# Channel attention with a two-layer feed-forward block: the softmax of batches 1 to 3 without TensorE, and other dues for the loads of the opening

## The chip, the core and the metric

The kernel runs on one core of a Trainium2 chip. Its engines are TensorE (PE, matrix products, with weight loads shown as PEld), VectorE (DVE), ScalarE (ACT), GpSimd (POOL) and SyncE (SP, which here issues every DMA). Each takes its instructions in order, and an instruction that waits holds up those behind it. The metric is the device time of one execution in microseconds (us), the median of several.

## The reference

Per batch, channels attend to channels, and the result goes through a feed-forward block with a piecewise activation. Cut to what matters:

```python
B, N, C = (4, 6080, 256)
qn = q / (np.linalg.norm(q, axis=1, keepdims=True) + 1e-06)
kn = k / (np.linalg.norm(k, axis=1, keepdims=True) + 1e-06)
s = kn.transpose(0, 2, 1) @ qn / tau            # 256 x 256 per batch
s = s - s.max(-1, keepdims=True)
a = np.exp(s)
a /= a.sum(-1, keepdims=True) + 1e-09
x = v @ a                                       # (4 * 6080) x 256
h = x @ w_in                                    # d_ff = 2048
g = np.where(h >= 1, h, np.where(h <= -1, 0.0, (h + 1) ** 2 / 4))
out = g @ w_out
```

`w_in` and `w_out` come as 64-bit floats.

## The kernel before

**What is computed where.** The two products v·a and ·w_in are merged: per batch W = a·w_in is made once, and h = v·W. Every operand of a large product is held as two fp32r parts, and a product is three matmuls (`mm3`, L465 to L469). h = v·W uses a Strassen form with seven products (`strassen`). N is cut into six column pairs per batch, and 2048 hidden channels into eight slices `i` of 256, so there are 48 groups per batch and 192 in all; a group is `h_ops` (the product and the activation) and `o_ops` (the product with `w_out`). Each group's h tiles leave PSUM through ACT and DVE and come back as operands of the `w_out` product.

**Batch 0's opening.** The Gram matrix kᵀq of batch 0 is made from chunks of 512 rows (1 MB each, the first of 256 rows) by plain fp32 matmuls in `big_chunk` (L848), from four buffers `kq_0` to `kq_3`. ACT squares each chunk and DVE adds the squares (L863, L864) for the norms. The first `EARLY` chunks of batch 1 go through the same loop, for the Gram matrix alone. Meanwhile the 64-bit weights are loaded and converted by ACT and DVE (`convert`), the first tiles of v are split (`make_V`), and W of batch 0 is made (`make_W`). `LOADS` places those loads: kind, index, due time, and the chunk load behind whose issue they may start.

**Later batches.** While the groups of one batch run, the rest of the next batch's Gram matrix is made from 256-row pieces (`gram_chunk`, 12 matmuls each on tile `kqs`) and the squares from `square_piece`. In group 40 of 0 to 47 (`SOFT_AT = 8`) comes `softmax(b + 1)`, and in groups 45 and 47 (`W_AT`) `make_W7`, which forms the next batch's W from tile `eT`, the transposed exponentials.

**Inside `softmax` before**, for all batches: DVE sums the squares, POOL takes the root (L527), DVE takes the reciprocals (L532). 1/|q| lies one channel to a partition and is wanted along the free axis in all partitions: DVE makes two diagonal matrices (L537), PE multiplies them by a matrix of ones (L544), DVE copies the result to `rq` (L547). Then scaling (L550), row maxima (L553), exponentials on ACT (L559), four transposes on PE (L569), and for batches 1 to 3 two copies from PSUM to `sf_mem` on ACT (L584), sums on POOL (L675) and the split into `eT` by ACT and DVE (L679, L681).

**What sets the order.** Nothing is issued as it is written: each operation is given to `Order` with an engine, an assumed length, the buffers it reads and writes, and a due time. `Order.run` walks through assumed times and, per engine, takes among the operations that can start the one with the earliest due; if none can start at once, the one that can start first. An urgent one (batch 0's norms and softmax) counts as startable up to `SOON` us ahead, so that the engine waits for it. The result is a fixed order for each engine. So a changed due can move instructions all over the program. Buffers, and with them what a load must wait for, are picked in the same walk.

Of the kernel before, what the change touches and what calls it, by code (L numbers as in the profile page):

```python
# [9 lines left out]
F32 = mybir.dt.float32  # L10
# [5 lines left out]
P = 128  # L16
# [31 lines left out]


URGENT = -1000.0  # L50
SOON = 0.6


class Op:
# [161 lines left out]
def pool_us(n):  # L216
# [20 lines left out]
W_AT = (3, 1)
SUMS_AT = (18, 21, 24, 27)  # L240
SOFT_AT = 8


HEAD = (2,)
KQ0, KQ1 = -12.0, 3.7


LOADS = (("in", 0, 42, 7), ("out", 0, 34, 2), ("in", 1, 42, 5), ("out", 2, 42, 4),
         ("v", 0, 52, 10), ("in", 2, 56, 7), ("out", 4, -46, 6), ("out", 6, 34, 6))


@with_exitstack
def channel_attention_moe(ctx: ExitStack, tc: tile.TileContext, kq, kqT, vT, tau, w_in, w_out, outT):
# [258 lines left out]
    def softmax(b, due):  # L512

        st = sts[b]
        c = st.col = buf("cols")
        col = lambda a, n: c.ap[:, a:a + n]
        ssq, nrm, rn = lambda: col(0, 4), lambda: col(4, 4), lambda: col(8, 4)
        nmax, sums, rs = lambda: col(12, 2), lambda: col(14, 2), lambda: col(16, 2)
        st.rs = rs
        V = nc.vector  # L520
        if b == 0:
            op("DVE", 0.2, lambda: V.tensor_copy(ssq(), st.pt.ap[:, :4]), r=[st.pt], w=[c], due=due)
        else:
            op("DVE", 0.2, lambda: V.tensor_reduce(
                out=ssq(), in_=st.ssq.ap[:, :4 * NCW].rearrange("p (a k) -> p a k", k=NCW), axis=AX.X, op=ALU.add),
               r=[st.ssq], w=[c], due=due)
        op("POOL", 1.0, lambda: nc.gpsimd.tensor_tensor(out=nrm(), in0=ssq(), in1=half, op=ALU.pow), w=[c], due=due)  # L527
        op("DVE", 0.1, lambda: V.tensor_scalar(out=nrm(), in0=nrm(), scalar1=1e-6, scalar2=None, op0=ALU.add), w=[c],
           due=due)
        op("DVE", 0.1, lambda: V.tensor_scalar(out=nrm()[:, :CT], in0=nrm()[:, :CT], scalar1=tau_sb, scalar2=None,  # L530
                                              op0=ALU.mult), w=[c], due=due)
        op("DVE", 0.1, lambda: V.reciprocal(rn(), nrm()), w=[c], due=due)  # L532
        q, s = buf("rq"), buf("sf")
        dg = lambda ct: s.ap[:, ct]
        sv = lambda it: s.ap.rearrange("p (t j) f -> p t (j f)", t=4)[:, it]
        for ct in range(CT):
            op("DVE", 0.25, lambda ct=ct: V.tensor_scalar(out=dg(ct), in0=ident,  # L537
                                                         scalar1=rn()[:, CT + ct:CT + ct + 1], scalar2=None,
                                                         op0=ALU.mult), r=[c], w=[s], due=due)
        z = buf("Z")  # L540

        def scales():
            for ct in range(CT):
                nc.tensor.matmul(z.ap[:, ct * P:(ct + 1) * P], lhsT=ones, rhs=dg(ct), start=True, stop=True)  # L544

        op("PE", 0.7, scales, r=[s], w=[z], due=due + 3)
        op("DVE", 0.42, lambda: V.tensor_copy(q.ap, z.ap[:, :C]), r=[z], w=[q], due=due + 3)  # L547
# [14 lines left out]
        if b == 0:  # L562
            touch(IDENTITY_SAT240, [s], due + 6.1)
        z2 = buf("Z")

        def transposes():
            for it in range(CT):
                for jt in range(CT):
                    nc.tensor.transpose(z2.ap[:, (jt * CT + it) * P:(jt * CT + it + 1) * P],  # L569
                                        sv(it)[:, jt * P:(jt + 1) * P], ident)  # L570

        op("PE", 0.6, transposes, r=[s], w=[z2], due=due + 8)
        if b == 0:
            st.eT = buf("eT")
            eT = lambda a: st.eT.ap[:, a * CT * C:(a + 1) * CT * C].rearrange("p (j c) -> p j c", j=CT)
            zz = lambda: z2.ap.rearrange("p (j c) -> p j c", j=CT)
            op("ACT", act_us(512), lambda: nc.scalar.copy(eT(0), zz()), r=[z2], w=[st.eT], due=due + 9)
            op("DVE", dve_us(512), lambda: V.tensor_tensor(out=eT(1), in0=zz(), in1=f32(eT(0)),
                                                          op=ALU.subtract), r=[z2], w=[st.eT], due=due + 9)
        else:  # L580
            f = s
            st.eT = buf("eT")
            for jt in range(CT):
                op("ACT", act_us(256), lambda jt=jt: nc.scalar.copy(  # L584
                    f.ap[:, OUT_[jt], :], z2.ap[:, jt * C:(jt + 1) * C].rearrange("p (i c) -> p i c", i=CT)),
                   r=[z2], w=[f], due=due + 9)
# [377 lines left out]
```

## Time and profile before

| | before |
|---|---|
| median of 3 runs | 2162.06 us (2161.85 to 2165.43) |
| the profiled execution's own time | 2162.27 us |
| its span in the profile | 2160.5 us |
| ACT busy | 1589.3 us (74%) |
| POOL busy | 246.5 us (11%) |
| bytes moved by DMA | 369.48 MB, mean 171 GB/s |

The span runs from the first to the last instruction; 1.8 us of the execution lie around it. Shares are of the span. In the timelines that follow, the columns are start, length, engine, line, operation, tiles, shape and count, and in brackets the idle time ahead of it and what ended that. A matmul's shown length reaches past the start of the next one, so its cost is read from start to start. A matmul of plain fp32 operands (L848, L544, L569) shows up as two instructions.

### The profile page before, as it was taken

The page shows a single profiled execution, that of the slowest core. Times are in us where ns is not written, and L with a number is a line of the kernel's source. Part 1 is how long each engine was busy: PE and PEld are TensorE (multiplying, and loading weights), DVE is VectorE, ACT ScalarE, POOL GpSimd, SP SyncE. Part 2 cuts the span into 40 slices and gives each one's busy share as a digit, 9 for nine tenths or more (in the row PEclk, how much of TensorE's full clock was granted, in tenths as well). Part 3 has the DMA queues.
Part 4 walks back from the last instruction along what each step waited for, and adds up shares of the span by engine and source line. Part 5 has one row for each costly group of instructions (what it writes and reads, how often), then busy time and mean ns, then how long its engine had stood idle before and what let it go on. Part 6 is the DMA issues. An engine that isn't in the chain of part 4 may idle for free.

```text
span 2160.5 us, 27947 instructions
## 1 busy us (share of the span) xinstructions
PE 2150.3 (100%) x9904; PEld 1804.1 (84%) x9904; DVE 1791.0 (83%) x2917; ACT 1589.3 (74%) x2809; POOL 246.5 (11%) x260
## 2 busy tenths in 40 slices
PE   9999999999999999999999999999999999999999
PEld 7888888888888888888888888888888888888888
DVE  7898888888798888888889888888888887778776
ACT  6687777777788777777777877777777767777776
POOL 0320020100131001000023000000012201001000
PEclk9999999999999999999999999999999999999999
DMA  9755466454665444544456445354455532332331
GB/s 382 289 188 174 144 219 219 164 179 144 200 232 182 171 154 159 181 163 159 173 185 222 172 163 182 144 202 143 150 184 190 185 124 91 128 127 96 121 120 36
DMA packets 115340, 369.48 MB, mean 171 GB/s; under 512 B 10496, under 2 KB 40192, under 8 KB 112768
## 3 DMA queue, kind: packets, MB, share of 16 engines
q1 hardware_dynamic: 115200, 367.70, 48.5%
q8 instruction: 78, 1.28, 0.2%
q14 instruction: 62, 0.51, 0.1%
HBM read 297.67 MB, written 69.99 MB: 170 GB/s over the span
## 4 chain that ended last, share of the span: by engine, by line
PE 96%; DVE 1%; DMA 0%; issue 0%; POOL 0%; ACT 0%; SPq 0%; DVEq 0%; ACTq 0%
PE bank L468 95%; DMA wop_d<-win_mem 0%; PE bank L848 0%; POOL t L719 0%; DVE v L728 0%; DVE v L726 0%; DVE win_mem L406 0%; DVE x L771 0%; PE bank L544 0%; PE bank L569 0%; DVE u_mem L399 0%; DVE wout L406 0%; DVE bank L622 0%; ACT v L725 0%; DVE mh_mem L626 0%
## 5 line engine op out<-in xcount | busy, mean ns | idle before, releaser
L468 PE MATMUL bank<-x,wout 128*128 128x512 f32 (+1 forms) x3948 | 1014.7, 388 | 0.0
L468 PEld LDWEIGHTS bank<-x,wout 128*128 128x128 f32 x3948 | 738.9, 188 | 146.7 <-DVE x L771 0.2
L468 PE MATMUL bank<-v,w_mem 128*128 128x512 f32 (+1 forms) x3264 | 850.1, 388 | 1.5 <-DVE v L728 0.8
L468 PEld LDWEIGHTS bank<-v,w_mem 128*128 128x128 f32 x3264 | 610.0, 188 | 125.4 <-DVE v L728 1.9
L763 ACT ACTIVATE u_mem<-bank 128x512 f32<-128x512 f32 (+1 forms) x576 | 341.8, 593 | 269.0 <-PE bank L468 259.1
L767 DVE TENSOR_TENSOR u_mem<-bank,u_mem 128x512 f32<-128x512 f32 (+1 forms) x576 | 390.6, 679 | 126.6 <-ACT u_mem L765 125.1
L765 ACT ACTIVATE u_mem<-u_mem 128x512 f32<-128x512 f32 (+1 forms) x768 | 469.1, 625 | 7.2
L771 DVE TENSOR_TENSOR x<-u_mem,x 128x512 fp32r<-128x512 f32 (+1 forms) x658 | 459.8, 706 | 11.4 <-ACT x L769 7.3
L769 ACT CAST x<-u_mem 128x512 fp32r<-128x512 f32 (+1 forms) x284 | 173.8, 615 | 78.7 <-DVE u_mem L767 78.2
L622 DVE TENSOR_TENSOR bank<-bank,mh_mem 128x512 f32<-128x512 f32 (+1 forms) x198 | 137.0, 692 | 96.4 <-PE bank L468 95.9
L468 PE MATMUL bank<-x,w_mem 128*128 128x512 f32 (+1 forms) x768 | 208.5, 388 | 0.0
L468 PE MATMUL bank<-g,wout 128*128 128x512 f32 (+1 forms) x660 | 183.4, 387 | 0.0
L719 POOL TENSOR_TENSOR t<-raw_mem 128x512 f32<-128x512 f32 (+1 forms) x48 | 66.8, 1392 | 890.0 <-DMA raw_mem<-vT 294.3
L468 PEld LDWEIGHTS bank<-x,w_mem 128*128 128x128 f32 x768 | 143.7, 188 | 28.8 <-DVE bank L622 0.2
L770 DVE CAST x<-u_mem 128x512 fp32r<-128x512 f32 (+1 forms) x374 | 159.5, 435 | 8.5 <-DVE u_mem L767 0.5
L626 DVE TENSOR_TENSOR mh_mem<-bank,mh_mem 128x512 f32<-128x512 f32 (+1 forms) x198 | 135.4, 684 | 37.4 <-PE bank L468 32.5
L617 ACT COPY mh_mem<-bank 128x512 f32<-128x512 f32 (+1 forms) x198 | 115.3, 582 | 65.1 <-PE bank L468 62.6
L767 DVE TENSOR_TENSOR u_mem<-mh_mem,u_mem 128x512 f32<-128x512 f32 (+1 forms) x192 | 136.4, 711 | 13.3 <-ACT u_mem L765 13.0
L468 PEld LDWEIGHTS bank<-g,wout 128*128 128x128 f32 x660 | 123.5, 188 | 24.5 <-DVE g L771 0.2
L619 ACT COPY bank<-bank 128x512 f32<-128x512 f32 (+1 forms) x198 | 113.3, 572 | 33.8 <-PE bank L468 28.3
L763 ACT ACTIVATE u_mem<-mh_mem 128x512 f32<-128x512 f32 (+1 forms) x192 | 119.0, 620 | 7.0 <-DVE mh_mem L626 6.8
L719 POOL TENSOR_TENSOR t<-raw_mem,t 128x512 f32<-128x512 f32 (+1 forms) x48 | 67.3, 1402 | 460.5 <-DVE v L728 369.2
(104 smaller groups left out, 1452.8 us busy)
## 6 DMA issues: line engine op xcount, KB each, us to landing
w_mem<-w_d SPq DMA_DIRECT2D x160, 896.0 KB, 4.6
raw_mem<-kqT SPq DMA_DIRECT2D x60, 512.0 KB, 6.1
w_d<-w_mem SPq DMA_DIRECT2D x32, 896.0 KB, 4.5
raw_mem<-kq SPq DMA_DIRECT2D x53, 512.0 KB, 5.5
raw_mem<-vT SPq DMA_DIRECT2D x40, 512.0 KB, 6.5
outT<-y_mem SPq DMA_DIRECT2D x80, 256.0 KB, 2.6
kq<-kq SPq DMA_DIRECT2D x19, 1024.0 KB, 9.0
win_mem<-wop_d SPq DMA_DIRECT2D x21, 512.0 KB, 5.7
```

The lines of the kernel that those rows point to most:

```text
L468: nc.tensor.matmul(out, lhsT=lhs(a), rhs=rhs(c), start=start and m == 0, stop=stop and m == 2, skip_group_check=skip)
L617: op("ACT", act_us(n), lambda: nc.scalar.copy(m5.ap[:, :n], a.ap[:, :n]), r=[a], w=[m5], due=early)
L619: op("ACT", act_us(n), lambda: nc.scalar.copy(a.ap[:, :n], z.ap[:, :n]), r=[z], w=[a], due=early)
L622: op("DVE", dve_us(n), lambda: nc.vector.tensor_tensor(out=bb.ap[:, :n], in0=z.ap[:, :n], in1=m5.ap[:, :n], op=ALU.add), r=[z, m5], w=[bb] ...
L626: op("DVE", dve_us(n), lambda: nc.vector.tensor_tensor(out=h22.ap[:, :n], in0=z.ap[:, :n], in1=m5.ap[:, :n], op=ALU.add), r=[z, m5], w=[h2 ...
L719: op("POOL", pool_us(n), lambda: nc.gpsimd.tensor_tensor(out=tt(x), in0=a(), in1=c(), op=ALU.subtract), r=r, w=[ts[x]], due=due + d, gates ...
L763: op("ACT", act_us(n), lambda: nc.scalar.activation(us(), src(), IDENTITY_SAT240, scale=240.0), r=[h], w=[u], due=d_sat)
L765: op("ACT", act_us(n), lambda: nc.scalar.activation(us(), us(), AF.Square, bias=0.5, scale=1.0 / 480.0), w=[u], due=d_sq)
L767: op("DVE", dve_us(n), lambda: nc.vector.tensor_tensor(out=us(), in0=src(), in1=us(), op=ALU.max), r=[h], w=[u], due=d_max)
L769: op("ACT", act_us(n), lambda: nc.scalar.copy(t.ap[:, 0, :n], us()), r=[u], w=[t], due=d_hi, other=("DVE", dve1_us(n), lambda: nc.vector.t ...
L770: other=("DVE", dve1_us(n), lambda: nc.vector.tensor_copy(t.ap[:, 0, :n], us())) if g >= FIRST else None)
L771: op("DVE", dve_us(n), lambda: nc.vector.tensor_tensor(out=t.ap[:, 1, :n], in0=us(), in1=f32(t.ap[:, 0, :n]), op=ALU.subtract), r=[u], w=[ ...
```

## The change

For batches 1 to 3 the spreading of 1/|q| goes through memory: SP stores the 256 reciprocals (4 bytes each) to a DRAM row `rn_d`, and loads that row into all partitions of `rq`. The exponentials are transposed in blocks of 32 x 32 by DVE into a `u` buffer, stored by eight DMAs that put the blocks in their places in `e_d` (256 runs of 128 bytes each), and loaded by two DMAs into `sf_mem`, where the copies from PSUM went. The two PE steps, the copy to `rq`, and the two ACT copies per batch go. Batch 0 keeps them. Beside it, planner numbers change: `SOON`, the number of early chunks of batch 1 (8 to 9), from which group on DVE may take ACT's casts, and dues and gates of several loads.

```diff
-SOON = 0.6
+SOON = 0.3
...
-EARLY = 8
+EARLY = 9
-FIRST = 0
+FIRST = 4
...
-SLACK = 0.0
-WOP_DUE, W_DUE, TAKE_DUE = -48, -14, -20
-GRAM_END = 0
-KQS_J = (2, 3)
+SLACK = 0
+WOP_DUE, W_DUE, TAKE_DUE = -60, -14, -20
+GRAM_END = 1
+KQS_J = (4, 5)
 W_AT = (3, 1)
-SUMS_AT = (18, 21, 24, 27)
-SOFT_AT = 8
+SUMS_AT = (20, 23, 28, 31)
+SOFT_AT = 9
...
-KQ0, KQ1 = -12.0, 3.7
+KQ0, KQ1 = -17.0, 3.2
-LOADS = (("in", 0, 42, 7), ("out", 0, 34, 2), ("in", 1, 42, 5), ("out", 2, 42, 4),
-         ("v", 0, 52, 10), ("in", 2, 56, 7), ("out", 4, -46, 6), ("out", 6, 34, 6))
+LOADS = (("in", 0, 40, 13), ("out", 0, 50, 4), ("in", 1, 32, 7), ("out", 2, 14, 5),
+         ("v", 0, 92, 13), ("in", 2, 54, 7), ("out", 4, 8, 8), ("out", 6, 2, 5))
...
+    rn_dram = [dram.tile([1, C], F32, name=f"rn_d{b}") for b in range(B)]
+    eT_dram = [dram.tile([CT * P, C], F32, name=f"e_d{b}") for b in range(B)]
...
         q, s = buf("rq"), buf("sf")
+        if b == 0:
...
+        else:
+            rd = Buf(ap=rn_dram[b])
+            op("SP", 0.07, lambda: nc.sync.dma_start(
+                out=rn_dram[b].rearrange("o (a p) -> p (o a)", p=P), in_=rn()[:, CT:2 * CT]), r=[c], w=[rd],
+               due=due, size=P * 128)
+            load(q, lambda: rn_dram[b].broadcast_to([P, C]), lambda: q.ap, due, P * C * 4, r=[rd])
...
         else:
             f = s
+            x, ed = buf("u"), Buf(ap=eT_dram[b])
+            for it in range(CT):
+                op("DVE", dve_us(256), lambda it=it: V.transpose(out=x.ap[:, it * C:(it + 1) * C], in_=sv(it)), r=[s], w=[x],
+                   due=due + 8)
+
+            def blocks():
+                for a in range(4):
+                    for it in range(CT):
+                        nc.sync.dma_start(
+                            out=eT_dram[b].rearrange("(m j) (t a i) -> j t a m i", j=32, t=CT, a=4)[:, it, a],
+                            in_=x.ap[a * 32:(a + 1) * 32, it * C:(it + 1) * C].rearrange("j (m i) -> j m i", i=32))
+
+            def rows():
+                for jt in range(CT):
+                    nc.sync.dma_start(out=f.ap[:, OUT_[jt], :],
+                                      in_=eT_dram[b][jt * P:(jt + 1) * P].rearrange("p (t c) -> p t c", t=CT))
+
+            op("SP", 0.56, blocks, r=[x], w=[ed], due=due + 8, size=P * 2048)
+            op("SP", 0.14, rows, r=[ed], w=[f], due=due + 8, size=P * 2048)
             st.eT = buf("eT")
-            for jt in range(CT):
-                op("ACT", act_us(256), lambda jt=jt: nc.scalar.copy(
-                    f.ap[:, OUT_[jt], :], z2.ap[:, jt * C:(jt + 1) * C].rearrange("p (i c) -> p i c", i=CT)),
-                   r=[z2], w=[f], due=due + 9)
             split_f(f, st.eT, due + 8, view=e_view)
```

Because the walk starts from other numbers, nearly every engine's order differs somewhere. Three places matter below.

On SP, between the reciprocals and the transposed exponentials of batch 1, where `w_d` are stored W tiles loaded back and `outT` is the output. Before:

```order
L374 DMA w_mem<-w_d_1_143 128x1792
L374 DMA w_mem<-w_d_2_144 128x1792
L374 DMA w_mem<-w_d_3_145 128x1792
L814 DMA outT<-y_mem 128x512
L374 DMA w_mem<-w_d_4_146 128x1792
L814 DMA outT<-y_mem 128x512 x3
```

On SP at the same place after the change:

```order
L376 DMA w_mem<-w_d_1_143 128x1792
L553 DMA rn_d_135<-cols_75 128x2x1
L376 DMA w_mem<-w_d_2_144 128x1792
L376 DMA rq<-rn_d_135 128x256
L376 DMA w_mem<-w_d_3_145 128x1792
L838 DMA outT<-y_mem 128x512
L599 DMA e_d_139<-u_mem 32x8x32 x8
L376 DMA w_mem<-w_d_4_146 128x1792
L838 DMA outT<-y_mem 128x512
L605 DMA sf_mem<-e_d_139 128x2x128 x2
L838 DMA outT<-y_mem 128x512 x2
```

Twelve issues come in between. The load of `rq` stands behind a load of a W tile, and the last two stand behind another and behind an output store.

On DVE in the same stage after the change, from the second block transpose on (`mh_mem`, `u_mem`, `bank` and `x` belong to the groups' h tiles):

```order
L593 STREAM_TRANSPOSE u_mem<-sf_mem 128x256
L650 TENSOR_TENSOR mh_mem<-bank_115,mh_mem 128x480
L593 STREAM_TRANSPOSE u_mem<-sf_mem 128x256
L612 TENSOR_SCALAR cols_75<-cols_75 128x2
L791 TENSOR_TENSOR u_mem<-bank_108,u_mem 128x480
L614 RECIPROCAL cols_75<-cols_75 128x2
L794 CAST g_94<-u_mem 128x480
L795 TENSOR_TENSOR g_94<-u_mem,g_94 128x480
```

And the end of that stretch on DVE after the change:

```order
L650 TENSOR_TENSOR mh_mem<-bank_114,mh_mem 128x480
L795 TENSOR_TENSOR x_683<-u_mem,x_683 128x480
L791 TENSOR_TENSOR u_mem<-bank_109,u_mem 128x480
L794 CAST x_700<-u_mem 128x480
L795 TENSOR_TENSOR x_700<-u_mem,x_700 128x480
L705 TENSOR_TENSOR eT<-sf_mem,eT 128x896
L791 TENSOR_TENSOR u_mem<-mh_mem,u_mem 128x480
L794 CAST x_700<-u_mem 128x480
L646 TENSOR_TENSOR bank_109<-bank_115,mh_mem 128x480
```

Between the second block transpose and the split of `eT` (L705) stand 21 instructions, and the sum into a PSUM bank (L646) stands three behind the split. Before, no DVE transpose was there, and the split of `eT` followed the PE transposes.

On PE in the opening, from the last chunk of batch 0 on (`bank_114` is batch 0's Gram matrix, `bank_113` batch 1's). Before:

```order
L848 MATMUL bank_114<-kq_0_81 128x256 x4
L848 MATMUL bank_113<-kq_1_82 128x256 x8
L848 MATMUL bank_113<-kq_2_83 128x256 x2
L870 MATMUL bank_115<-ones,mh_mem 128x1 x8
L848 MATMUL bank_113<-kq_2_83 128x256 x6
L544 MATMUL bank_115<-sf_mem,ones 128x128 x2
L848 MATMUL bank_113<-kq_3_84 128x256 x8
```

On PE at the same place after the change:

```order
L872 MATMUL bank_114<-kq_0_81 128x256 x4
L872 MATMUL bank_113<-kq_1_82 128x256 x8
L872 MATMUL bank_113<-kq_2_83 128x256 x4
L894 MATMUL bank_115<-ones,mh_mem 128x1 x8
L872 MATMUL bank_113<-kq_2_83 128x256 x4
L872 MATMUL bank_113<-kq_3_84 128x256 x4
L547 MATMUL bank_115<-sf_mem,ones 128x128 x2
L872 MATMUL bank_113<-kq_3_84 128x256 x4
```

Between the norms (`ones,mh_mem`) and the spreading of batch 0's 1/|q| (`sf_mem,ones`) now stand eight matmuls of chunks in place of six.

More of the change, by code (lines that the diff above doesn't have):

```diff
@@ L533, in softmax, with scales @@
         q, s = buf("rq"), buf("sf")
-        dg = lambda ct: s.ap[:, ct]
         sv = lambda it: s.ap.rearrange("p (t j) f -> p t (j f)", t=4)[:, it]
[L536 to L542, printed above, removed]
-            for ct in range(CT):
-                nc.tensor.matmul(z.ap[:, ct * P:(ct + 1) * P], lhsT=ones, rhs=dg(ct), start=True, stop=True)
-        op("PE", 0.7, scales, r=[s], w=[z], due=due + 3)
-        op("DVE", 0.42, lambda: V.tensor_copy(q.ap, z.ap[:, :C]), r=[z], w=[q], due=due + 3)
+        if b == 0:
+            dg = lambda ct: s.ap[:, ct]
+            for ct in range(CT):
+                op("DVE", 0.25, lambda ct=ct: V.tensor_scalar(out=dg(ct), in0=ident,
+                                                             scalar1=rn()[:, CT + ct:CT + ct + 1], scalar2=None,
+                                                             op0=ALU.mult), r=[c], w=[s], due=due)
+            z = buf("Z")
+            def scales():
+                for ct in range(CT):
+                    nc.tensor.matmul(z.ap[:, ct * P:(ct + 1) * P], lhsT=ones, rhs=dg(ct), start=True, stop=True)
+            op("PE", 0.7, scales, r=[s], w=[z], due=due + 3)
+            op("DVE", 0.42, lambda: V.tensor_copy(q.ap, z.ap[:, :C]), r=[z], w=[q], due=due + 3)
+        else:
[4 more added lines that the diff above has]
+            load(q, lambda: rn_dram[b].broadcast_to([P, C]), lambda: q.ap, due, P * C * 4, r=[rd])
         gm = (lambda: st.g.ap) if b else (lambda: st.g.ap.rearrange("p (i c) -> p i c", i=CT))
@@ L563, in softmax, with transposes @@
             touch(IDENTITY_SAT240, [s], due + 6.1)
-        z2 = buf("Z")
-        def transposes():
-            for it in range(CT):
-                for jt in range(CT):
-                    nc.tensor.transpose(z2.ap[:, (jt * CT + it) * P:(jt * CT + it + 1) * P],
-                                        sv(it)[:, jt * P:(jt + 1) * P], ident)
-        op("PE", 0.6, transposes, r=[s], w=[z2], due=due + 8)
-        if b == 0:
+        if b == 0:
+            z2 = buf("Z")
+            def transposes():
+                for it in range(CT):
+                    for jt in range(CT):
+                        nc.tensor.transpose(z2.ap[:, (jt * CT + it) * P:(jt * CT + it + 1) * P],
+                                            sv(it)[:, jt * P:(jt + 1) * P], ident)
+            op("PE", 0.6, transposes, r=[s], w=[z2], due=due + 8)
             st.eT = buf("eT")
@@ L581, in softmax @@
             f = s
+            x, ed = buf("u"), Buf(ap=eT_dram[b])
[4 more added lines that the diff above has]
+                for a in range(4):
+                    for it in range(CT):
+                        nc.sync.dma_start(
+                            out=eT_dram[b].rearrange("(m j) (t a i) -> j t a m i", j=32, t=CT, a=4)[:, it, a],
+                            in_=x.ap[a * 32:(a + 1) * 32, it * C:(it + 1) * C].rearrange("j (m i) -> j m i", i=32))
+            def rows():
+                for jt in range(CT):
+                    nc.sync.dma_start(out=f.ap[:, OUT_[jt], :],
+                                      in_=eT_dram[b][jt * P:(jt + 1) * P].rearrange("p (t c) -> p t c", t=CT))
+            op("SP", 0.56, blocks, r=[x], w=[ed], due=due + 8, size=P * 2048)
+            op("SP", 0.14, rows, r=[ed], w=[f], due=due + 8, size=P * 2048)
             st.eT = buf("eT")
-            for jt in range(CT):
-                op("ACT", act_us(256), lambda jt=jt: nc.scalar.copy(
-                    f.ap[:, OUT_[jt], :], z2.ap[:, jt * C:(jt + 1) * C].rearrange("p (i c) -> p i c", i=CT)),
-                   r=[z2], w=[f], due=due + 9)
             split_f(f, st.eT, due + 8, view=e_view)
```

## The prediction

> **What bounds the kernel now.** I read the page's engine totals and the chain that ended last, then what PE waited for, then the same chain in order of time around batch 1's softmax.
>
> ```profile
> span 2160.5 us, 27947 instructions
> PE 2150.3 (100%) x9904; PEld 1804.1 (84%) x9904; DVE 1791.0 (83%) x2917; ACT 1589.3 (74%) x2809; POOL 246.5 (11%) x260
> PE 96%; DVE 1%; DMA 0%; issue 0%; POOL 0%; ACT 0%; SPq 0%; DVEq 0%; ACTq 0%
> ```
>
> PE is busy all through and carries the chain. A busy PE isn't yet PE at its peak, so the next view asks whether it ever waits:
>
> ```profile
> PE bank L848 <- DMA kq<-kq: 3.0, 2, 1.7
> PE bank L875 <- POOL half L289: 1.5, 1, 1.5
> PE bank L468 <- DVE v L728: 0.8, 1, 0.8
> PE bank L544 <- DVE sf_mem L537: 0.7, 1, 0.7
> PE bank L468 <- DVE mh_mem L626: 0.5, 1, 0.5
> ```
>
> Six waits, 6.5 us in all. So time goes away in two ways only: PE gets less to do, or one of these waits shrinks. Anything taken off DVE, ACT or POOL is worth nothing by itself, but they and SP can bring new waits.
>
> **What leaves PE.** The chain in order of time (start, length, what), around batch 1's softmax:
>
> ```profile
> 94.75 420.56 PE bank L468 x1926
> 515.31 0.45 PE bank L544 x4
> 515.75 9.99 PE bank L468 x45
> 525.75 0.44 PE bank L569 x4
> ```
>
> The spreading and the transposes stand on the path with 0.45 and 0.44 us, with PE busy on both sides. Batches 2 and 3 have the same pieces. Three batches save 3 x 0.89 = **2.7 us**.
>
> **What comes to PE.** One more early chunk is 8 matmuls in plain fp32, and two pieces of 12 matmuls in fp32r go later.
>
> ```profile
> 89.92 1.73 PE bank L848 x8
> ```
>
> ```profile
> 1169.73 1.36 PE L468 MATMUL bank<-kqs 128*128 128x256 f32 x10
> 1170.93 0.86 PE L468 MATMUL bank<-x,wout 128*128 128x512 f32 x3
> ```
>
> Eight instructions, which are four such matmuls, take 1.73 us; a chunk takes 3.46. Ten matmuls of the pieces take 1.20 from start to start, 24 take 2.88. That adds **0.6 us**.
>
> **The opening.** PE's timeline, and the busy share of the DMA engines in the first 60 us (last two numbers):
>
> ```profile
> 5.29 29.15 PE L848 MATMUL bank<-kq 128*128 128x256 f32 x120 [1.75 <-DMA kq<-kq]
> 35.68 20.22 PE L848 MATMUL bank<-kq 128*128 128x256 f32 x92 [1.24 <-DMA kq<-kq]
> 60.96 0.68 PE L544 MATMUL bank<-sf_mem,ones 128*128 128x128 f32 x4 [0.68 <-DVE sf_mem L537]
> 80.98 1.42 PE L468 MATMUL bank<-v,w_mem 128*128 128x512 f32 x5 [0.75 <-DVE v L728]
> 0.00:60.00 60.00, 55.55 (x242) 46.64 (x242) 45.18 (x51) 34.25 (x37) 2.77 (x9) 1.00 0.97 383
> ```
>
> The 1.75 is the first chunk's landing; the loads up to it keep their places, so it stays. The other three can go, 1.24 + 0.68 + 0.75 = 2.67 us:
> - The 1.24 is the ninth chunk of batch 0. Adding up the sizes of the loads in SP's order, 12.6 MB are issued up to its end now and 11.8 after. At the 383 GB/s of that row it lands 2 us earlier.
> - The 0.68 is PE at the spreading, before DVE has the diagonals. Two more matmuls of a chunk, 0.87 us, come ahead of it and cover it.
> - The 0.75 is the first tile of v. Its second load now ends at 24.5 MB of the order in place of 28.7, some 11 us earlier at that rate.
>
> But DMA is at 97%, so a load moved forward moves another back. The third chunk of batch 1 now ends at 21.9 MB in place of 21.1, 2.1 us later, and the eleventh of batch 0 0.3 MB later. PE reaches both sooner than before. New waits lie between 0 (PE may come no earlier than they do) and 2.8 us (both delays in full). I take 0.9, nearer the lower end, because PE came to no chunk but the ninth too early in the trace. The opening gives 2.67 - 0.9 = **1.8 us**. Dropping `SOON` acts on urgent operations alone, so it belongs to this term.
>
> **The new round trips.** No row shows a store of 4-byte or 128-byte runs, a block transpose on DVE, or a chain of store and load. The nearest rows: issues with KB each and median us to landing; two stretches of SP's timeline (start, length of the issue).
>
> ```profile
> w_mem<-w_d SPq DMA_DIRECT2D x160, 896.0 KB, 4.6
> outT<-y_mem SPq DMA_DIRECT2D x80, 256.0 KB, 2.6
> raw_mem<-raw_d SPq DMA_DIRECT2D x48, 128.0 KB, 4.2
> wop_d<-kqs SPq DMA_DIRECT2D x8, 512.0 KB, 5.8
> tau_sb<-tau SPq DMA_DIRECT2D x1, 0.5 KB, 3.0
> ```
>
> ```profile
> 56.50 0.90 SPq L427 DMA_DIRECT2D wop_d<-win_mem  x2
> 515.96 0.34 SPq L814 DMA_DIRECT2D outT<-y_mem  x1
> ```
>
> *1/|q|.* The order on DVE from the reciprocals to the first scaling is nearly that of before up to the 512-wide subtraction at 506.36:
>
> ```profile
> 497.20 0.17 DVE L532 RECIPROCAL cols<-cols 128x4 f32<-128x4 f32 x1
> 506.36 0.69 DVE L771 TENSOR_TENSOR x<-u_mem,x 128x512 fp32r<-128x512 f32 x1
> ```
>
> So DVE comes to the scaling some 9.7 us after the reciprocals. The trip: 0.4 to issue and 3.0 to land (the 128 elements of `tau`), then on SP, which holds everything behind until then, 0.4 to issue `rq`, and 4.6 behind the W tile's load issued ahead of it: 8.4. DVE waits for nothing, with 1.3 us to spare. The W tile's load behind is delayed by up to 3 us; it is wanted a round of groups later.
>
> *The exponentials.* The same stretch of DVE in the trace of before, with POOL's and ACT's steps:
>
> ```profile
> 515.79 0.42 DVE L547 COPY rq<-bank 128x256 f32<-128x256 f32 x1
> 516.65 0.65 DVE L626 TENSOR_TENSOR mh_mem<-bank,mh_mem 128x480 f32<-128x480 f32 x1
> 528.54 2.37 POOL L675 TENSOR_TENSOR sf_mem<-sf_mem 128x128 f32<-128x128 f32 x4 [25.12 <-ACT sf_mem L584]
> 529.37 0.80 DVE L771 TENSOR_TENSOR x<-u_mem,x 128x480 fp32r<-128x480 f32 x1
> 531.93 0.95 ACT L679 CAST eT<-sf_mem 128x896 fp32r<-128x896 f32 x1
> 533.13 1.08 DVE L681 TENSOR_TENSOR eT<-sf_mem,eT 128x896 fp32r<-128x896 f32 x1
> 534.13 0.65 DVE L622 TENSOR_TENSOR bank<-bank,mh_mem 128x480 f32<-128x480 f32 x1
> 553.97 0.85 PE L468 MATMUL bank<-win_mem,eT 128*128 128x512 f32 x3
> ```
>
> The first product that reads `eT` starts 20 us behind the split, so a late `eT` costs nothing by itself; what stands behind it on ACT and DVE may. After the change the second block transpose follows the row of 516.65, so it ends near 517.7 (0.4 us, as the 256-wide row of 515.79), and DVE is at the split of `eT` after the row of 529.37, at 530.2. The trip: eight issues of 0.45, 3.6; landing 3.0; two issues, 0.9; landing between 2.6 and 4.2; POOL 2.4; ACT 1.0. That is 13.5 to 15.1 us, and DVE waits until 531.2 to 532.8. Behind it stand the split (1.1), two short instructions (1.0, by rows of this kind) and the sum into the PSUM bank, which PE needs and which DVE began at 534.1 before. It would begin between 533.3 and 534.9, 0.8 too late at worst. ACT holds its cast in the same way. With PE's sequence a round ahead, I take 0.1 us a batch, **0.3 us**. The lower end is 0; the upper is the late mechanism below. The 9 DVE instructions that go and the 6 transposes that come are off the path.
>
> **The rest** of the reordering has 2,000 us in which PE waited once, 0.5 us (`mh_mem`). I take 0, from -0.5 to +2 for a few waits of that size.
>
> **Sum.** -2.7 + 0.6 - 1.8 + 0.3 = -3.6 us, from the profiled 2162.27 to 2158.7. That execution is 0.2 over the median shown, so 2158.5 for the median. About 0.2%, 4.3 us, is what a measurement of this kernel can tell from no change, so the boundary of faster is 2157.7: very near.
>
> **Rivals.**
> 1. *The opening gives its waits back in full*, with no new one, and the round trips cost nothing: -2.7 + 0.6 - 2.67 = -4.8, with the late 0.5 -5.3: 2156.8 to 2157.3. For it: PE's only waits on chunks were two, and loads run ahead by up to four buffers. Against: the 97%.
> 2. *The saturated DMA takes the opening's gain*: waits of 2.8 in place of 0.9, and 1 us more for the extra chunk's own MB (2.7 us at 383 GB/s, partly hidden): 2161. Faster still, within 0.2%.
> 3. *The transposed exponentials come late*, and ACT's and DVE's orders hold the groups' work behind them. From about 1 us of lateness PE stands, once per batch. If the store lands as late as the slowest in steady state (5.8) and the load as `rq` was taken behind a W tile (4.6), it is 3.2 us later than the worse end above; with both at 6, 4.8. At 4 us in three batches: +12, 2170. It decides from 2.6 us a batch ((4.3 + 3.6) / 3), where the time passes 2166.4. For it: both hops are of runs that no row has. Against: the `tau` row, and a DMA share of 0.28 in this stage:
>
> ```profile
> 510.00:520.00 10.00, 10.00 (x48) 8.46 (x47) 8.34 (x18) 6.73 (x13) 0.00 (x0) 1.00 0.28 110
> ```
>
>    The Trainium skill speaks for this rival: "VectorE: DVE Perf Modes", section "The three transpose paths", warns that a plain DMA copy that transposes by strides is 19 times slower than the transpose engine's. By that rule the 256 KB, 0.7 us at 383 GB/s, would take 13 us, some 9 more than taken here, and three batches would end near 2183 (an estimate). No run here shows it yet; here the runs are 128 bytes and not single elements, because DVE has turned the blocks.
> 4. *PE is not what the removed work waited for*: the 2.7 us come back as waits for DVE, which is 83% busy. 2161.2. Against: PE's waits.
>
> **How the numbers follow.** The forecast 0.40; rival 1 0.35; rivals 2 and 4 together 0.13; rival 3 0.12. Faster by over 0.2% is rival 1: 0.35. Within: 0.40 + 0.13 = 0.53. Slower is rival 3: 0.12. The range reaches from 2155.2 (rival 1, with 1.6 us of small gaps of PE beside it) to 2164 (the forecast with the rest's +2 and 1 us a batch of lateness); rival 3 is left out.
>
> **What would show it.** PE without L544 and L569 instructions after 100 us; waits of PE in the opening near 0.9 beside the first chunk's; a timeline of SP in which the eight stores take 3.6 us; DVE's wait at the scaling 0, and at the split of `eT` 1 to 2.6 us. The prediction is wrong if PE shows waits behind `eT` or `mh_mem` near 520, 1050 and 1580, or new waits for chunks of over 3 us.

## The result, and the profile after

The changed kernel takes **2179.05 us** (median of 6 runs, 2177.17 to 2181.45) where before takes 2162.39 (6 runs, 2161.85 to 2165.43): a ratio of 1.0075 with a 95% interval of 1.0062 to 1.0088, 16.7 us slower. The forecast was 2158.5 with a range up to 2164. The profiled execution took 2179.38 us.

The page of the changed kernel, engine totals, then what PE waited for (us in total, times, longest):

```profile
span 2177.6 us, 27933 instructions
PE 2153.8 (99%) x9872; PEld 1802.9 (83%) x9872; DVE 1776.3 (82%) x2867; ACT 1605.9 (74%) x2844; POOL 246.0 (11%) x260
```

```profile
PE bank L470 <- DVE u_mem L791: 7.2, 3, 5.1
PE bank L470 <- ACT bank L643: 4.4, 4, 1.6
PE bank L872 <- DMA kq<-kq: 3.1, 4, 1.7
PE bank L470 <- ACT sf_mem L689: 2.2, 1, 2.2
PE bank L899 <- POOL half L289: 1.5, 1, 1.5
PE bank L470 <- DVE eT L587: 0.9, 1, 0.9
```

PE has 32 matmul instructions fewer, as foretold, and waits some 20 us in place of 6.5. The waits for `u_mem` (L791) and for a bank (L643) are new. Both are work of the groups, and no part of the softmax: DVE and ACT came late to it because they stood elsewhere.

To add up such losses with all that follows from them (behind the longest wait here TensorE ran slower for 2.5 us more, as the last section shows) I use one measure for every kernel: the distance from each matmul's start to the next, less the median distance of that shape in the trace of before, summed where the two differ by over 0.06 us. By it PE's pure work fell from 2142.6 to 2140.5 us, and the loss rose from 12.0 to 30.8. By stretch, in us (500-560, 1030-1095 and 1570-1630 hold the softmaxes of batches 1 to 3):

| kernel | median, us | 0-60 | 60-100 | 100-500 | 500-560 | 1030-1095 | 1570-1630 | rest |
|---|---|---|---|---|---|---|---|---|
| before | 2162.4 | 8.5 | 2.4 | 0.1 | 0.0 | 0.0 | 0.0 | 1.0 |
| changed | 2179.1 | 6.6 | 5.4 | 2.2 | 9.9 | 2.8 | 3.0 | 1.0 |
| numbers_alone | 2173.8 | 6.6 | 3.9 | 3.0 | 0.2 | 1.6 | 1.5 | 6.0 |
| soft_alone | 2175.9 | 8.3 | 2.7 | 0.1 | 2.2 | 5.8 | 4.6 | 4.2 |
| store_out | 2170.1 | 6.9 | 5.5 | 1.6 | 4.1 | 1.7 | 1.8 | 0.5 |
| trips_out | 2162.2 | 6.5 | 5.5 | 1.1 | 0.0 | 0.0 | 0.0 | 0.5 |
| rn_128 | 2168.4 | 6.3 | 4.0 | 1.3 | 3.1 | 1.3 | 1.5 | 0.4 |
| both_planned | 2162.3 | 6.7 | 3.9 | 2.0 | 0.3 | 0.0 | 0.0 | 0.5 |
| v0_dve | 2157.8 | 7.0 | 0.5 | 2.2 | 0.0 | 0.0 | 0.0 | 0.5 |
| opening_of_before | 2161.4 | 8.3 | 2.5 | 0.1 | 0.0 | 0.7 | 0.0 | 0.7 |

(The medians come from several chips, on which before had 2162.4 to 2163.7; ratios below are to runs on the same chip. The losses are those of the one profiled execution, which lies up to 2.2 us off the median: 2166.3 for rn_128, 2160.2 for opening_of_before.) The loss of the changed kernel lies in the three softmaxes (15.7 us) and behind the opening (60 to 500: 7.6 in place of 2.5).

**1/|q|, batch 1**, in the timeline of the changed kernel (start, length, engine, line; in brackets the idle time ahead):

```profile
501.38 0.17 DVE L534 RECIPROCAL cols<-cols 128x4 f32<-128x4 f32 x1
501.58 0.38 SPq L553 DMA_DIRECT2D rn_d<-cols  x1
510.29 0.32 SPq L376 DMA_DIRECT2D rq<-rn_d  x1
517.33 0.48 DVE L559 SCALAR_TENSOR_TENSOR sf_mem<-gacc,cols,rq 128x256 f32<-128x256 f32 x1 [6.12 <-DMA rq<-rn_d]
518.45 0.62 ACT L793 CAST x<-u_mem 128x512 fp32r<-128x512 f32 x1 [6.26 <-DVE u_mem L791]
518.47 1.97 PE L470 MATMUL bank<-v,w_mem 128*128 128x480 f32 x4 [5.07 <-DVE u_mem L791]
```

DVE is free for the scaling at 511.2, 9.7 us behind the end of the reciprocals, as forecast. But SP could issue the load only at 510.29, and it landed at 517.3. DVE stands 6.1 us, ACT's cast behind DVE's next maximum 6.3, and PE 5.1. The issues of the page (KB each, median us to landing):

```profile
rn_d<-cols SPq DMA_DIRECT2D x3, 1.0 KB, 8.7
rq<-rn_d SPq DMA_DIRECT2D x3, 128.0 KB, 5.7
e_d<-u_mem SPq DMA_DIRECT2D x24, 32.0 KB, 1.7
sf_mem<-e_d SPq DMA_DIRECT2D x6, 128.0 KB, 5.4
```

The store of 1 KB lands in 8.7 us; I had taken 3.0. The load of `rq` lands in 5.7; I had taken 4.6.

**The exponentials, batch 1**, same timeline:

```profile
529.58 3.88 SPq L599 DMA_DIRECT2D e_d<-u_mem  x8
534.05 0.38 SPq L838 DMA_DIRECT2D outT<-y_mem  x1
534.74 1.51 SPq L605 DMA_DIRECT2D sf_mem<-e_d  x2
539.92 0.59 ACT L835 COPY y_mem<-bank 128x512 f32<-128x512 f32 x1 [2.81 <-DMA outT<-y_mem]
544.47 0.94 ACT L703 CAST eT<-sf_mem 128x896 fp32r<-128x896 f32 x1 [1.55 <-POOL sf_mem L699]
545.91 0.93 PE L470 MATMUL bank<-v,w_mem 128*128 128x480 f32 x3 [1.61 <-ACT bank L643]
```

ACT is held twice: by an output copy whose buffer comes free only when an output store lands that SP issued behind the eight stores, and by the cast of `eT`. The bank copy that PE needs (L643) stands behind the cast.

### The profile page after: what moved, and what is told of

It is laid out like the page before. It is cut to its first block, busy times and chain, and to the rows that moved or that the text cites. A ratio compares the mean times of both kernels' runs of the same rounds, so it can differ in the third digit from the quotient of the medians.

```text
span 2177.6 us, 27933 instructions
## 1 busy us (share of the span) xinstructions
PE 2153.8 (99%) x9872; PEld 1802.9 (83%) x9872; DVE 1776.3 (82%) x2867; ACT 1605.9 (74%) x2844; POOL 246.0 (11%) x260
## 5 line engine op out<-in xcount | busy, mean ns | idle before, releaser
L791 DVE TENSOR_TENSOR u_mem<-bank,u_mem 128x512 f32<-128x512 f32 (+1 forms) x576 | 390.7, 680 | 143.0 <-ACT u_mem L789 141.6
L793 ACT CAST x<-u_mem 128x512 fp32r<-128x512 f32 (+1 forms) x319 | 194.9, 615 | 94.3 <-DVE u_mem L791 93.0
L646 DVE TENSOR_TENSOR bank<-bank,mh_mem 128x512 f32<-128x512 f32 (+1 forms) x198 | 137.1, 693 | 92.6 <-PE bank L470 91.4
L794 DVE CAST x<-u_mem 128x512 fp32r<-128x512 f32 (+1 forms) x339 | 150.9, 453 | 7.4
L791 DVE TENSOR_TENSOR u_mem<-mh_mem,u_mem 128x512 f32<-128x512 f32 (+1 forms) x192 | 136.6, 712 | 13.9 <-ACT u_mem L789 13.7
L643 ACT COPY bank<-bank 128x512 f32<-128x512 f32 (+1 forms) x198 | 113.5, 573 | 36.2 <-PE bank L470 30.9
```

Of the source, the lines that this page charges most:

```text
L643: op("ACT", act_us(n), lambda: nc.scalar.copy(a.ap[:, :n], z.ap[:, :n]), r=[z], w=[a], due=early)
L646: op("DVE", dve_us(n), lambda: nc.vector.tensor_tensor(out=bb.ap[:, :n], in0=z.ap[:, :n], in1=m5.ap[:, :n], op=ALU.add), r=[z, m5], w=[bb] ...
L791: op("DVE", dve_us(n), lambda: nc.vector.tensor_tensor(out=us(), in0=src(), in1=us(), op=ALU.max), r=[h], w=[u], due=d_max)
L793: op("ACT", act_us(n), lambda: nc.scalar.copy(t.ap[:, 0, :n], us()), r=[u], w=[t], due=d_hi, other=("DVE", dve1_us(n), lambda: nc.vector.t ...
L794: other=("DVE", dve1_us(n), lambda: nc.vector.tensor_copy(t.ap[:, 0, :n], us())) if g >= FIRST else None)
```

## The experiments

**The two halves.** First the change was taken apart: the new softmax on the numbers of before, the new numbers with the old softmax, and the changed kernel with one of the two trips put back on PE.

```diff
 # soft_alone, against the changed kernel: each number as before; numbers_alone the other way round
-SOON = 0.3
+SOON = 0.6
-EARLY = 9
+EARLY = 8
...
 # rn_pe; tr_pe does the same ahead of transposes()
-        if b == 0:
-            dg = lambda ct: s.ap[:, ct]
+        dg = lambda ct: s.ap[:, ct]
...
-        else:
-            rd = Buf(ap=rn_dram[b])
```

> The new softmax of batches 1 to 3 with all the numbers of before (EARLY 8, SOON 0.6, the old loads). Theory (the landing of the 1 KB store of 1/|q|, taken as 3.0 us and 8.7 us in the trace, stops DVE and then PE, and the trip of the exponentials stops it a little more): before's 2162.4, less 2.7 for the removed PE work, plus about 10 us for the stops at 1/|q| and about 5 for those at eT: 2172 to 2177. Rival (the new numbers carry the loss, the softmax is free): 2159 to 2161. Rival (each carries half): 2168 to 2170.

> The new numbers (EARLY 9, SOON 0.3, the new loads and due times) with the softmax of before. Theory: the ninth early chunk costs 0.6 us, the opening wins its two waits but loses at POOL's differences of v and at eT near 68 and 81 us, so 2162 to 2167. Rival (the new numbers carry the loss): 2174 to 2180. Prediction's own sum for this part alone: 0.6 - 1.8, 2161.

> The changed kernel with 1/|q| of all batches spread by PE again; the exponentials still go by block transposes and DRAM. Theory: the 10 us of stops at the scaling go and 1.4 us of PE work come back: 2169 to 2172. Rival (the transposed exponentials carry the loss): 2178 to 2181, no change or a little slower than the changed kernel.

> The changed kernel with the exponentials of all batches transposed by PE again; 1/|q| of batches 1 to 3 still goes through DRAM. Theory: the stops at eT, about 1.5 us a batch, go and 1.3 us of PE work come back: 2174 to 2177. Rival (the transposed exponentials carry the loss): 2163 to 2168.

Measured: soft_alone 2175.89 us (ratio 1.0061, 1.0046 to 1.0076); numbers_alone 2173.82 (1.0048, 1.0033 to 1.0063); rn_pe 2174.12 (1.0049, 1.0033 to 1.0066); tr_pe 2174.92 (1.0055, 1.004 to 1.007). soft_alone and tr_pe came as the theory said, rn_pe 2 us above it; the numbers alone were 7 us worse than it allowed, at the edge of the rival's range. And the halves, 12.2 and 10.2 us above before, add up to more than the whole, 16.7. PE's waits in numbers_alone:

```profile
PE bank L468 <- ACT sf_mem L665: 2.2, 1, 2.2
PE bank L848 <- DMA kq<-kq: 2.2, 2, 1.8
PE bank L468 <- DVE x L771: 1.6, 3, 0.6
PE bank L875 <- POOL half L289: 1.5, 1, 1.5
PE bank L468 <- ACT bank L619: 1.3, 1, 1.3
```

Many small waits, and in the table 6.0 us of them in "rest", where the changed kernel has 1.0. A new order can bring waits of its own, as here, in soft_alone (4.2 in "rest") and, by the same measure, in rn_pe (4.9) and tr_pe (4.8). It need not: opening_of_before, further down, has 0.7 there. So putting one part of a planned kernel alone on another order does not price that part safely. The experiments that follow therefore keep the changed kernel's order.

**The trips left out, in the same order.** store_out issues no store of 1/|q|; the scaling uses constants put into `rn_d` long before. trips_out leaves out the eight stores of the exponentials too, and reads constants from `e_d`.

```diff
-            op("SP", 0.07, lambda: nc.sync.dma_start(out=rn_dram[b]..., in_=rn()[:, CT:2 * CT]), ...)
+            op("SP", 0.07, lambda: None, ...)
-            op("SP", 0.56, blocks, ...)
+            op("SP", 0.56, lambda: None, ...)
```

> The changed kernel, in its order on every engine, without the store of 1/|q| (batches 1 to 3 scale by constants put in DRAM long before; the load of rq stays where it stands). In the trace of the changed kernel PE loses 9.9 us between 500 and 560, 2.8 between 1030 and 1095 and 3.0 between 1570 and 1630 against the durations of before. Theory (the store's 8.7 us are what stops DVE at the scaling): the large gap near 513 and those near 1055 and 1589 go, about 10 us with the cold clock behind the first; 2168 to 2170. Rival (the load of rq behind a W tile is late by itself, with or without the store): 2176 to 2179.

> As the one without the store of 1/|q|, and without the eight stores of the exponentials in each of batches 1 to 3 too; the two loads of sf stay where they stand (batches 1 to 3 then use the wrong exponentials). Theory (the two trips make up nearly all of the 15.7 us in the three stretches around the softmax): 2163 to 2166, with PE's gaps in those stretches under 1.5 us together. Rival (the order on the engines itself, not the trips, makes the gaps): 2170 or more.

Measured: store_out 2170.07 us (1.0032, 1.002 to 1.0044), trips_out 2162.17 (0.9998, 0.9989 to 1.0007). So of the 16.9 us between the changed kernel and trips_out, 9.0 hang on the store of 1/|q| and 7.9 on the stores of the exponentials, and with both gone PE loses nothing in the three stretches. What the change costs there is the two trips; the order by itself costs nothing in these stretches. The split depends on what is taken out first: in the changed kernel's own trace the losses behind the scaling are 10.4 us and those behind the exponentials 5.2, and without the first stop the second grows to 7.6. In batch 1 ACT then reaches the output copy earlier and waits longer for it, 3.8 us in place of 2.8; the wait at the cast stays as it was. In store_out, ACT's timeline:

```profile
532.98 0.59 ACT L841 COPY y_mem<-bank 128x512 f32<-128x512 f32 x1 [3.79 <-DMA outT<-y_mem]
537.51 0.94 ACT L709 CAST eT<-sf_mem 128x896 fp32r<-128x896 f32 x1 [1.54 <-POOL sf_mem L705]
```

**A store in longer runs.** rn_128 lets DVE transpose the 32 small columns, so that 1/|q| leaves in 8 runs of 128 bytes; order and planner as in the changed kernel.

```diff
+            V.transpose(out=colsT, in_=c.ap)      # behind the reciprocals, b > 0
-                out=rn_dram[b].rearrange("o (a p) -> p (o a)", p=P), in_=rn()[:, CT:2 * CT])
+                out=rn_dram[b].rearrange("o (a q i) -> (o a) q i", a=CT, i=32)[a], in_=colsT[8 + CT + a::32, :])
```

> The changed kernel in its order, but DVE turns the 32 columns of small numbers by a block transpose behind the reciprocals, and 1/|q| is stored as 8 runs of 128 bytes by two issues in place of 256 runs of 4 bytes. Theory (the 256 runs of 4 bytes are what lands late): the store lands in 2 to 3 us, DVE's wait at the scaling falls from 6.1 to under 1 us, and the time is that without the store, 2168 to 2171. Rival (any store that small lands late here, because it goes behind a W tile's load of 896 KB): landing 6 us or more, 2175 to 2179.

Measured: 2168.41 us (1.0022, 1.0013 to 1.0032), the time without the store. SP's wait for the landing, in rn_128 and in the changed kernel (total, times, longest):

```profile
SPq L379 <- DMA rn_d<-colsT: 2.6, 3, 1.0
```

```profile
SPq L376 <- DMA rn_d<-cols: 24.3, 3, 9.5
```

The same kilobyte at the same place of the queue: at most 1.0 us of waiting in place of 9.5. So it is the form of the store, not its place.

**Which form.** Two probes set small stores that nobody waits for into the kernel before. The first had one of each kind; the second, 48 stores, has eight of each of six kinds.

```diff
+            lambda: (flat(pr[0])[:2 * P].rearrange("(a p) -> p a", p=P), half[:, :2]),
+            lambda: (flat(pr[1])[:2 * P].rearrange("(p a) -> p a", p=P), half[:, :2]),
+            lambda: (pr[2][:, ::32], half[:, :2]),
+            lambda: (flat(pr[3])[:P].rearrange("(p a) -> p a", p=P), half[:, :1]),
+            lambda: (pr[4][:, :1], half[:, :1]),
+            lambda: (pr[5][:, :32], ident[:, :32]),
```

In this order, as `pa_d` to `pf_d`: 256 runs of 4 bytes side by side; 128 of 8 side by side; 256 of 4, 128 bytes apart; 128 of 4 side by side; 128 of 4, 256 bytes apart; 128 of 128 bytes, 256 bytes apart.

> The kernel before, with six small stores ahead of loads of batch 2's squares, nobody waiting for them: 256 runs of 4 bytes side by side (as the store of 1/|q|), 128 runs of 8 bytes side by side, 256 runs of 4 bytes 128 bytes apart, 8 runs of 128 bytes, 2 runs of 512 bytes, 128 runs of 4 bytes side by side. Theory (the number of 4-byte runs sets the landing): 7 to 10 us for the 256 runs of 4 bytes, near or far; about half for the 128 of 8 and of 4 bytes; 1.5 to 3 us for 8 and 2 runs. Rival (all runs into the same few lines of DRAM wait for one another): side by side slow, 128 bytes apart fast. Rival (what is ahead on the queue): all alike.

> The kernel before, with 48 small stores ahead of the loads of the squares of batches 2 and 3, eight of each of six kinds, nobody waiting for them. The first probe had one of each kind: 10.9 us for 256 runs of 4 bytes side by side, 6.3 for 128 runs of 8 bytes side by side, 6.4 for 256 runs of 4 bytes 128 bytes apart, 9.6 for 128 runs of 4 bytes side by side. Theory A (runs that share a few lines of DRAM wait for one another): in the median 8 to 11 us for 256 and for 128 runs of 4 bytes side by side, 4 to 6.5 for 256 runs 128 bytes apart, for 128 runs 256 bytes apart and for 128 runs of 128 bytes, with 8 bytes side by side between. Theory B (the number of runs sets it): 256 runs near or far alike, 128 runs of 4 bytes near or far alike and about half. Theory C (what is ahead on the queue sets it): all six within 1.5 us.

In the first, the four kinds of which the trace has a landing took 10.9 (256 of 4 bytes, near), 6.3 (128 of 8, near), 6.4 (256 of 4, apart) and 9.6 us (128 of 4, near); it took 2166.22 us in its one run. The second (2179.49 us, one run: 48 small stores in the way of the loads cost much) has, as medians of eight:

```profile
pc_d<-half SPq DMA_DIRECT2D x8, 1.0 KB, 5.5
pd_d<-half SPq DMA_DIRECT2D x8, 0.5 KB, 10.3
pe_d<-half SPq DMA_DIRECT2D x8, 0.5 KB, 5.3
pf_d<-ident SPq DMA_DIRECT2D x8, 16.0 KB, 5.1
pa_d<-half SPq DMA_DIRECT2D x8, 1.0 KB, 10.5
pb_d<-half SPq DMA_DIRECT2D x8, 1.0 KB, 7.1
```

My first theory, that the number of runs sets the landing, falls: 128 runs of 4 bytes take as long as 256, and the same 128 runs a little apart take half. All six medians lie where theory A put them: it is 4-byte writes side by side. Single stores scatter (7.8 to 12.7 us for the two near kinds of 4 bytes, 3.7 to 9.2 for the two far ones). The 5 us of the others here are probably the price of that place, behind what else SP had issued, since the 128-byte runs of `e_d` landed in 1.7 us in the changed kernel; that was not tried. What the near writes add is some 5 us.

**The plan told of the trips.** both_planned does all the work of the changed kernel; only the planner's assumed lengths differ.

```diff
-               due=due, size=P * 128)                          # the store of 1/|q|
+               due=due, size=P * 128, slack=6.0)
-            load(q, ..., P * C * 4, r=[rd])
+            load(q, ..., P * C * 4, r=[rd], slack=2.5)
-            op("SP", 0.56, blocks, ...)
-            op("SP", 0.14, rows, ..., size=P * 2048)
+            op("SP", 3.9, blocks, ...)
+            op("SP", 1.5, rows, ..., size=P * 2048, slack=1.7)
```

> The changed kernel, the same work, with the planner told of the durations in the trace: landing of the store 9.0 and of rq 5.5 us in place of 3.0, the eight issues 3.9 us in place of 0.56, the two loads 1.5 and landing 4.7. Its order differs near the three softmaxes alone. Theory (a wait that the plan doesn't know of): DVE and ACT have other work ahead of the scaling and the split, PE's gaps near 513, 544, 1055, 1079, 1589 and 1613 shrink to under 1 us each; 2164 to 2169. Rival (the trips are too long for the room that the softmax has before its first product): the gaps turn up later, at products that wait for eT; 2174 to 2180.

Measured: 2162.34 us (0.9997, 0.9988 to 1.0007), better than expected. The trip is as long as ever, but now DVE and ACT have work until it ends:

```profile
rn_d<-cols SPq DMA_DIRECT2D x3, 1.0 KB, 9.2
```

```profile
DVE sf_mem L559 <- DMA rq<-rn_d: 0.6, 1, 0.6
```

The landing is 9.2 us, and DVE waits for `rq` 0.6 us in three batches, where it waited 10.3 in the changed kernel.

**What the opening lost.** In both_planned PE still loses 3.9 us between 60 and 100. The timeline of both_planned, with POOL's four differences of the first tile of v, DVE beside them, and what follows the last:

```profile
64.11 1.22 DVE L398 SCALAR_TENSOR_TENSOR u_mem<-raw_mem,u_mem 128x1024 uint32<-128x1024 uint32 x1
65.29 1.27 POOL L743 TENSOR_TENSOR t<-raw_mem 128x512 f32<-128x512 f32 x1 [6.08 <-DMA raw_mem<-vT]
65.52 2.12 DVE L401 SCALAR_TENSOR_TENSOR u_mem<-raw_mem,u_mem 128x1024 uint32<-128x1024 uint32 x1
66.63 2.13 POOL L743 TENSOR_TENSOR t<-raw_mem,t 128x512 f32<-128x512 f32 x1
72.39 1.59 POOL L743 TENSOR_TENSOR t<-raw_mem 128x512 f32<-128x512 f32 x1 [3.63 <-DVE v L752]
77.06 0.69 DVE L752 TENSOR_TENSOR v<-t,v 128x512 fp32r<-128x512 f32 x1
...
77.89 4.52 POOL L743 TENSOR_TENSOR t<-raw_mem,t 128x512 f32<-128x512 f32 x1 [3.90 <-DVE v L752]
...
80.06 1.22 DVE L398 SCALAR_TENSOR_TENSOR u_mem<-raw_mem,u_mem 128x1024 uint32<-128x1024 uint32 x1
82.44 0.62 ACT L749 CAST v<-t 128x512 fp32r<-128x512 f32 x1 [4.91 <-POOL t L743]
82.96 0.47 ACT L689 ACTIVATE sf_mem<-bank,cols 128x256 f32<-128x256 f32 x1
83.48 0.72 PE L470 MATMUL bank<-v,w_mem 128*128 128x512 f32 x2 [2.23 <-ACT sf_mem L689]
```

One and the same operation takes 1.27 or 4.52 us. The last begins in an unbroken row of DVE instructions (77.06 to 81.28) and ends 1.1 us behind it; ACT holds the scaling of W (L689) behind the cast that waits for it, and PE waits for that. v0_dve keeps the order and lets DVE compute these four; before_v0 and opening_of_before_v0 make the same edit in the kernel before, and in opening_of_before (the softmax and slacks of both_planned, all other numbers of before).

```diff
-            ... nc.gpsimd.tensor_tensor(out=tt(x), in0=a(), in1=c(), op=ALU.subtract)
+            ... (nc.vector if (b, k) == (0, 0) else nc.gpsimd).tensor_tensor(...)
```

> The kernel with the planner told of the trips (2162.3 us), in its order, but the four differences of the first tile of v are computed by DVE at the places where POOL had them. In its trace PE stands 2.2 us at 81 us behind POOL's difference of 4.52 us, which starts while DVE works without a pause. Theory (POOL is held off by DVE's instructions; this wait is what the opening lost): the wait goes, DVE takes four times 0.7 us more, of which some delays other v tiles: 2159.5 to 2161.5. Rival (PE waits for DVE's work there in any case): 2162 to 2164, with the wait now behind DVE.

> The new softmax with the planner told of the trips, on the opening, the number of early chunks and all the other numbers of before. Theory (with the trips known the softmax costs nothing, and only the 2.7 us of PE work go): 2159 to 2161. Rival (each new order brings small waits of PE through the three batches, as the two halves of the change alone show): 2162 to 2170.

> The kernel before, in its order, with the four differences of the first tile of v computed by DVE in place of POOL. Its POOL difference at 76.2 us took 2.8 us beside DVE's stream and 1.3 to 1.6 elsewhere, and PE's only wait for that tile is 0.75 us, behind DVE. Theory (the gain of this edit on the planned kernel belongs to the new numbers, which put POOL's difference under DVE's stream on the path): within 1 us of before, 2161.5 to 2163.5. Rival (POOL's slow differences cost before as much): 2158 to 2160.

> The new softmax with the trips planned on the numbers and the opening of before (2161.4 us), with the same edit to the first tile of v. Theory: within 1 us of that kernel, 2160.4 to 2162.4. Rival: 2157 to 2159, and then the new opening brings nothing.

Measured: v0_dve 2157.75 us (0.9973, 0.9963 to 0.9983), better than expected and faster than both kernels; opening_of_before 2161.38 (0.999, 0.9981 to 0.9999), a little above the theory; before_v0 2160.43 (0.9989, 0.998 to 0.9997); opening_of_before_v0 2158.95 (0.9981, 0.9972 to 0.999). The differences in v0_dve (number, ns min/median/max), and all that PE still waits for over 0.3 us:

```profile
L743 DVE TENSOR_TENSOR t<-raw_mem x2: 682/683/684, 65.5 to 72.2; 128x512 f32<-128x512 f32 x2
L743 DVE TENSOR_TENSOR t<-raw_mem,t x2: 681/682/683, 67.5 to 77.3; 128x512 f32<-128x512 f32 x2
```

```profile
PE bank L872 <- DMA kq<-kq: 2.7, 3, 1.8
PE bank L899 <- POOL half L289: 1.5, 1, 1.5
```

The loss between 60 and 100 falls from 3.9 to 0.5. With the 2.2 us a second wait goes, which I had not foreseen: 0.9 us of PE for `eT` (L587) near 69. In both_planned DVE came to that instruction late, behind two that took 2.12 and 1.76 us beside POOL's differences; in v0_dve the same two take 1.20 and 0.68. The edit gains 0.24% on the new numbers and, against my theory, 0.1% on the opening of before too (there the same stretch loses 2.4 us without it and 0.4 with it): POOL's slow difference, 2.8 us in that trace, cost time as well. So the new opening made that loss larger, but did not begin it. And v0_dve and opening_of_before_v0 can't be told apart, as their intervals overlap: the new opening brings nothing that these runs show.

**Another plan.** best_128 is opening_of_before with the store of rn_128 and the planner told that it lands soon.

> As the one with the opening of before, with 1/|q| stored in 8 runs of 128 bytes and the planner told of its short landing (3.0 us, and rq 4.5). Theory: the same gain of 2.7 us, and the trip of 1/|q| gets shorter by 7 us than the plan with 4-byte runs has to allow: 2158.5 to 2161. Rival (small waits of a new order): 2162 to 2168.

Measured: 2162.34 us (0.9995, 0.9986 to 1.0004), in the rival's range. The shorter trip gave a new order, and in its profiled execution (2164.18 us, the longest of its 11) that one loses 5.3 us between 60 and 100 and 1.9 up to 500, far from any softmax. From opening_of_before it can't be told apart by the intervals.

## Why the prediction was wrong

The mechanism of the gain was right. Three terms of the sum were wrong: the two trips and the opening. A rival named the smaller part of the loss, the late exponentials; none named the larger, the late 1/|q|.

- **PE's work, -2.7 + 0.6: right.** PE's pure work fell by 2.1 us, and no L547 or L579 instruction stands behind batch 0.
- **The trip of 1/|q|, "DVE waits for nothing, with 1.3 us to spare": the step that failed.** The time at which DVE would come, 9.7 us, was right. The landing of the store, "3.0 to land (the 128 elements of `tau`)", was 8.7 us, and the load of `rq` took 5.7 in place of 4.6: 6.8 us more, where 1.3 were to spare, and DVE stood 6.1 in batch 1. `tau` was the row nearest in size, but it is a load, and this is 256 writes of 4 bytes side by side. I gave that landing one value, and even rival 3, on the other trip, went no further than 6 for a store. Cost 9.0 us.
- **The trip of the exponentials, 0.1 us a batch: mis-sized.** The pieces were near: 3.88 us for the eight issues (3.6 taken), 1.7 to land (3.0), 1.51 for two issues (0.9), 5.4 to land (2.6 to 4.2), POOL 2.45 (2.4), 15.8 from the first issue to the end of ACT's cast where 13.5 to 15.1 were worked out. What I priced was DVE's wait at the split, and that was 1.3 us, within the 1 to 2.6 forecast. ACT comes to its half first, and the bank copy for PE stands behind it. And I had not counted the output stores that SP holds behind the eight issues, for whose buffers ACT waits 2.8 us. Cost 7.9 us, 2.6 a batch: just the point that rival 3 gave as deciding. That rival, at 0.12, was right in kind for this share. The Trainium skill's warning in "VectorE: DVE Perf Modes", section "The three transpose paths", of plain copies 19 times slower (13 us by my estimate from it) is for a large innermost stride at the destination. With runs of 128 bytes it did not come about here: the eight stores took 3.88 us to issue and landed 1.7 us behind.
- **The opening, -1.8: wrong in sign.** Up to 60 us the loss did fall by 1.9, but most of that is TensorE reaching full speed earlier: 7 matmuls at the start run at about half speed there, 14 in before, 0.2 us each. That is luck: over the 17 traces of this case it is 6 to 14, with either opening. The new waits for chunks, 0.55, 0.38 and 0.45 us, add up to 1.4 where 0.9 was forecast, and ate most of the 1.24 and 0.68 that went. Between 60 and 100 it lost 3.0 more, of which 1.5 are slow matmuls behind the wait near 81; such matmuls follow that wait in only half of the traces that have it. The 0.75 at the first tile of v I had laid to its load; the load came earlier, as said, and POOL's last difference then fell under DVE's stream and took 4.52 us.
- **The rest, 0 (-0.5 to +2):** 2.1 us more between 100 and 500, the longest waits 0.5 and 1.1 us; the upper bound. Their cause was not tried.
- **The sum.** With the trips known to the plan the change is worth nothing that can be measured (2162.34): PE's 2.1 us are gained and 1.8 up to 60, and 3.4 more loss between 60 and 500 us takes most of that back. With the differences on DVE as well it is 2157.75, of which before gains 0.1% by the same edit. What the forecast left out is that the order had been planned with lengths as short as its own, so that nothing was there to cover the difference.

Not tried: the output stores moved out from behind the eight issues, and each of the two trips planned by itself.

## What to carry to other kernels

Where a fixed order is planned from assumed lengths, a new operation must first be measured in the form in which it will run: a few lengths taken too short cost 17 us here, and putting the measured ones into the plan, with the same work, brought all of it back. Price a new wait by every engine that meets it and by every queue behind it, not by the engine that you thought of first. And judge one part of a planned kernel only in an order that is held fixed; on another order the small waits of that order can hide it.

## What was not expected of the hardware

- In the second probe, stores of 4-byte runs side by side in DRAM land in 10.3 to 10.5 us, 128 and 256 runs alike; the same runs 128 or 256 bytes apart in 5.3 to 5.5; 8-byte runs side by side in 7.1; 128 runs of 128 bytes in 5.1. Why near ones wait was not tried.
- In both_planned, POOL's subtraction of 512 columns takes 1.29 us with no DVE instruction beside it (at 172.04) and 4.52 when it begins in an unbroken row of DVE instructions, which keep their usual lengths. The other way round, where POOL's began first (65.29), it took 1.27 and DVE's slowed down: L401 on 1024 columns took 2.12 us there and 1.20 in v0_dve, with no POOL beside it. The Trainium skill's "GPSIMD Engine Reference", section "1. Specifications", says that the two share their way to SBUF; the trace agrees.
- After the wait of 5.1 us in the changed kernel TensorE's next 12 matmuls start 0.40 to 0.57 us apart where 0.22 is usual, 2.5 us more. After the wait of 2.2 us near 81 it did so in four of the eight traces that have this wait (changed, store_out, trips_out, rn_pe), 1.2 to 1.7 us more within eight matmuls, and not in the other four (both_planned among them). The Trainium skill, "TensorE: Matmul & The Clock Gate", section "What's actually happening", names an idle window of about 3.4 us; a wait of 2.2 could cost the speed here.
